# Gated attention and a maxout feed-forward: seven block products on every superblock, half of the turns inside the couple, outputs issued by GpSimd

## The chip, the cores and the metric

The kernel runs on one core of a Trainium2 chip. Its time is the device time of one execution in microseconds; the number that counts is the median over several runs. TensorE is the matrix engine (PE, its weight loads PEld), VectorE is DVE, ScalarE is ACT, GpSimd is POOL, and SyncE (SP) only issues transfers here. Each engine works through its own queue in order, and waits on semaphores where it needs another engine's result.

## The reference

```python
# u, v: 8 x 3072 x 256, z: 8 x 3072 x 64, f32
scores = (1.0 / S) * np.matmul(z, z.transpose(0, 2, 1))
attn = np.maximum(scores, 0.0) ** 2
x = u * np.matmul(attn, v)
# x as 24576 tokens of 256
h1, h2 = x @ w1, x @ w2              # 256 x 1024 each
out = np.maximum(h1, h2) @ w_out     # 1024 x 256
```

Two identities are used by both kernels. The scores are symmetric, so only the blocks on and above the diagonal are computed. And max(h1, h2) = h2 + relu(h1 - h2), so that out = relu(x (w1 - w2)) w_out + x (w2 w_out), where w1 - w2 (`w15_sb`) and w2 w_out (`W2o_sb`) are made once.

## The kernel before

**Tiling.** A batch's 3072 tokens are 24 tiles of 128; four tiles make a group (512 tokens), two groups a *couple* (1024 tokens), so a batch has six groups and three couples c = 0, 1, 2. The attention matrix of a batch is 6 x 6 *blocks* of 512 x 512, kept in bf16 in 27 slots (`free`, `Block`); two by two blocks make a *superblock* (c, o), with blocks A11, A12, A21, A22.

**Scores.** `score_pair` computes half a block: two matmuls at the same time on the two halves of the array's rows (64 is the depth of z), two relus by ScalarE into `r_sb` (three buffers), and later, in `finish`, the square by VectorE into the block. A block above the diagonal is turned by a transposing transfer on SP's queue (`mirror`), which yields its mirror image; of a diagonal block only the upper triangle is computed (a *triangle* pair has less work) and the rest turned in place by three small transfers. A batch has 42 pairs; each couple of the loop issues 14 of them for later use, spread over its steps by `at_step`. `emit_pair(wait=6)` puts the square six steps behind its matmuls in program order.

**Attention times v.** In batch 0 the product is done plainly. From batch 1 on, a couple computes its 1024 x 256 outputs by a scheme of Strassen's kind: on a superblock off the diagonal, eight block products become seven, with sums of score blocks S1 to S4 and of v blocks (`combine_v`) made by VectorE beforehand. On the diagonal superblock the eight plain products stay. `ORDER` lists the products by two lanes, one for each half of the array's rows; one *step* is two matmuls, one per lane. A product is accumulated in one PSUM bank (`BANK`), half of it in one lane and half later in the other; a `nop` on another engine (`relay`) passes on that the first half is done. S1, S2, S3 are made before the couple; S4 overwrites A12 during the couple. The `after_...` functions add up the products in f32 on VectorE (`h_sb`) as they end, and so free the banks.

**Feed-forward.** `gate` multiplies the sums by u (turned by a transposing transfer, `turn_u`) into `xT`, on VectorE. `ff` then does a group: eight times two matmuls into `d_ps`, a relu into `g_sb` (numbers 2, 5 and 7 by VectorE, the others by ScalarE), then for each 128 tokens two matmuls with `W2o_sb` and eight with `w_out_sb` into `o_ps`, a copy by ScalarE into `o_sb` (two buffers) and an output transfer of 256 KB on ScalarE's queue. `d_ps`, `o_ps` and the score tiles share four PSUM buffers; the other four banks belong to the products.

**Order.** The program order is written out by hand. After the steps of couple i come the gates of couple i and the sums for couple i + 1 as a list of VectorE *tasks*, and then, in `second(i - 1, tasks)`, the feed-forward of the couple before. So TensorE has two groups of feed-forward to do while VectorE works on the tasks. `second` spreads the tasks over the feed-forward's matmuls by its `hook`:

```python
places = {(1, 0): 1, (1, 3): 1, (2, 0): 1, (2, 1): 1, (2, 2): 1, (2, 3): 1}
```

so that the relus of VectorE come between them in its queue.

## Time and profile before

| | |
|---|---|
| median of 3 runs | 950.33 us (946.04, 950.33, 955.08) |
| span of the profiled execution | 943.4 us |
| TensorE busy | 929.3 us, 7,706 matmuls |
| VectorE busy | 717.3 us |
| ScalarE busy | 552.8 us |
| GpSimd busy | 57.0 us |
| mean busy share of the 16 DMA engines | 60.4% transposing queue, 20.6% GpSimd's, 8.1% ScalarE's outputs |
| HBM read and written | 59.77 MB and 25.17 MB |

The profile is of one execution, and its span of 943.4 us is the time that the sums below are made against; the page gives no other time for that execution. The timed runs lie 2.6 to 11.7 us above the span. A busy share is an average; what a place costs is read from the timeline at that place.

### The profile page before, as it was taken

The page shows a single profiled execution, that of the slowest core. Times are in us where ns is not written, and L with a number is a line of the kernel's source. Part 1 is how long each engine was busy: PE and PEld are TensorE (multiplying, and loading weights), DVE is VectorE, ACT ScalarE, POOL GpSimd, SP SyncE. Part 2 cuts the span into 40 slices and gives each one's busy share as a digit, 9 for nine tenths or more (in the row PEclk, how much of TensorE's full clock was granted, in tenths as well). Part 3 has the DMA queues.
Part 4 walks back from the last instruction along what each step waited for, and adds up shares of the span by engine and source line. Part 5 has one row for each costly group of instructions (what it writes and reads, how often), then busy time and mean ns, then how long its engine had stood idle before and what let it go on. Part 6 is the DMA issues. An engine that isn't in the chain of part 4 may idle for free.

```text
span 943.4 us, 19492 instructions
## 1 busy us (share of the span) xinstructions
PE 929.3 (99%) x7706; PEld 517.5 (55%) x7706; DVE 717.3 (76%) x1158; ACT 552.8 (59%) x1062; POOL 57.0 (6%) x111
## 2 busy tenths in 40 slices
PE   8997999999999999999999999999999999999998
PEld 4454465554555555555546555465465554655555
DVE  6772588778887787987878869788688787885651
ACT  6793856556556566566565565655756657563333
POOL 3100000000000000000000000000000000000000
PEclk9998999999999999999999999999999999999999
DMA  9999999989999995998979999799979889985301
GB/s 190 148 201 210 164 209 157 133 162 186 148 166 143 159 205 119 174 160 159 185 127 157 164 173 182 119 180 151 172 165 134 172 158 174 153 156 106 80 24 67
DMA packets 388652, 146.00 MB, mean 155 GB/s; under 512 B 361936, under 2 KB 365904, under 8 KB 388560
## 3 DMA queue, kind: packets, MB, share of 16 engines
q1 hardware_dynamic: 359328, 90.09, 60.4%
q0 software_dynamic: 15408, 29.50, 20.6%
q10 hardware_dynamic: 13824, 25.17, 8.1%
q8 instruction: 60, 0.98, 0.5%
q14 instruction: 32, 0.26, 0.1%
HBM read 59.77 MB, written 25.17 MB: 90 GB/s over the span
## 4 chain that ended last, share of the span: by engine, by line
PE 91%; DVE 5%; ACT 1%; issue 1%; DMA 1%; SPq 0%; ACTq 0%; DVEq 0%
PE acc L829 44%; PE o_ps L448 16%; PE d_ps L420 15%; PE s_ps L201 7%; PE o_ps L440 4%; PE acc L259 4%; DVE xT L404 1%; DVE g_sb L428 1%; ACT r_sb L214 1%; DMA blk<-blk 1%; DVE h_sb L735 1%; DVE blk L311 1%; DVE blk L303 0%; DVE blk L307 0%; DVE blk L222 0%
## 5 line engine op out<-in xcount | busy, mean ns | idle before, releaser
L829 PE MATMUL acc<-blk,v_sb 64*128 64x512 bf16 x2544 | 467.1, 376 | 0.0
L214 ACT ACTIVATE r_sb<-s_ps 128x512 bf16<-128x512 f32 (+3 forms) x664 | 333.5, 554 | 127.3 <-PE s_ps L201 126.4
L829 PE MATMUL acc<-blk,vt 64*128 64x512 bf16 x1344 | 328.6, 376 | 0.0
L829 PEld LDWEIGHTS <-v_sb 64*128 64x128 bf16 x2544 | 183.7, 94 | 141.5 <-issue 4.6
L222 DVE TENSOR_TENSOR blk<-r_sb 128x1024 bf16<-128x1024 bf16 x251 | 171.1, 689 | 99.5 <-ACT r_sb L214 98.1
L448 PE MATMUL o_ps<-w_out_sb,g_sb 128*128 128x256 bf16 x1536 | 202.9, 273 | 1.2 <-DVE g_sb L428 0.4
L420 PE MATMUL d_ps<-xT,w_sb 128*128 128x512 bf16 x768 | 180.3, 382 | 5.2 <-ACT o_sb L456 3.9
L448 PEld LDWEIGHTS <-g_sb 128*128 128x128 bf16 x1536 | 150.0, 98 | 26.7 <-DVE g_sb L428 7.0
L829 PEld LDWEIGHTS <-vt 64*128 64x128 bf16 x1344 | 125.6, 94 | 70.7
L456 ACT COPY o_sb<-o_ps 128x512 f32<-128x512 f32 x96 | 56.3, 586 | 184.2 <-PE o_ps L448 174.5
L432 ACT ACTIVATE g_sb<-d_ps 128x512 bf16<-128x512 f32 x240 | 130.3, 599 | 56.8 <-PE d_ps L420 52.3
L420 PEld LDWEIGHTS <-w_sb 128*128 128x128 bf16 x768 | 73.4, 98 | 100.7 <-issue 24.7
L428 DVE TENSOR_SCALAR g_sb<-d_ps 128x512 bf16<-128x512 f32 x144 | 96.2, 685 | 42.6 <-PE d_ps L420 34.2
L201 PE MATMUL s_ps<-zT 64*128 64x512 bf16 (+3 forms) x672 | 124.1, 357 | 1.0 <-ACT zT L119 0.5
L735 DVE TENSOR_TENSOR h_sb<-h_sb,acc 128x512 f32<-128x512 f32 x147 | 96.9, 682 | 28.1 <-PE acc L829 27.4
L220 DVE TENSOR_TENSOR blk<-r_sb 128x512 bf16<-128x512 bf16 (+3 forms) x170 | 50.9, 324 | 41.8 <-ACT r_sb L214 40.7
L440 PE MATMUL o_ps<-W2o_sb,xT 128*128 128x256 bf16 x384 | 73.4, 273 | 0.0
L404 DVE SCALAR_TENSOR_TENSOR xT<-h_sb,uT 128x512 bf16<-128x512 f32 x96 | 63.3, 681 | 0.0
L201 PEld LDWEIGHTS <-zT 64*128 64x128 bf16 x672 | 35.1, 94 | 38.5 <-ACT zT L119 1.0
L259 PE MATMUL acc<-blk,v_sb 64*128 64x512 bf16 x384 | 50.6, 376 | 1.8 <-DVE blk L222 1.3
L311 DVE TENSOR_TENSOR blk<-blk,blk 128x2048 bf16<-128x2048 bf16 x42 | 51.4, 1223 | 1.2
L754 DVE TENSOR_TENSOR blk<-blk,blk 128x2048 bf16<-128x2048 bf16 x42 | 51.1, 1218 | 0.0
(53 smaller groups left out, 348.6 us busy)
## 6 DMA issues: line engine op xcount, KB each, us to landing
out_dram<-o_sb ACTq DMA_DIRECT2D x96, 256.0 KB, 2.8
un<-in_u_dram POOLq DMA_DIRECT2D x48, 256.0 KB, 6.8
v_sb<-in_v_dram POOLq DMA_DIRECT2D x21, 512.0 KB, 7.3
blk<-blk SPq DMA_TRANSPOSE x246, 5.5
zn<-in_z_dram POOLq DMA_DIRECT2D x21, 128.0 KB, 4.5
v_sb<-in_v_dram POOLq DMA_DIRECT2D x6, 256.0 KB, 7.1
blk<-in_moe_w_dram POOLq DMA_DIRECT2D x2, 512.0 KB, 6.2
uT<-un SPq DMA_TRANSPOSE x48, 3.4
```

The lines of the kernel that those rows point to most:

```text
L201: nc.tensor.matmul(s_ps[h][:, lo[h] :], zT[rows, z_at(b, blk * G + tiles[h]), :], zT[rows, q + lo[h] // P : q + G, :].rearrange("p t c -> ...
L214: nc.scalar.activation(o, s, AF.Relu)
L222: nc.vector.tensor_mul(a[:, k : k + 2, :], r, r)
L259: nc.tensor.matmul(a.out(acc[half, dc]), v_at(b, t, dc)[rows], a.moving(rows, j), start=first, stop=last,)
L404: lambda dc=dc: nc.vector.scalar_tensor_tensor(out=x[:, dc, :].rearrange("p (t r) -> p t r", r=P), in0=hs[dc].rearrange("p (t r) -> p t r" ...
L420: nc.tensor.matmul(d_ps, w15_sb[:, kc, ts(nb, P)], xT[:, kc, :], start=(kc == 0), stop=(kc == KD - 1),)
L428: nc.vector.tensor_single_scalar(out=g_sb[:, nb, :], in_=d_ps, scalar=0.0, op=ALU.max)
L432: nc.scalar.activation(g_sb[:, nb, :], d_ps, AF.Relu)
L440: nc.tensor.matmul(o_ps[:, t, :], xT[:, dc, ts(t0 + t, P)], W2o_sb[:, dc, :], start=(dc == 0), stop=False,)
L448: nc.tensor.matmul(o_ps[:, t, :], g_sb[:, nb, ts(t0 + t, P)], w_out_sb[:, nb, :], start=False, stop=(nb == KF - 1),)
L735: nc.vector.tensor_add(out, a, b_)
L829: mm = nc.tensor.matmul(a.out(acc[name]), w()[rows], a.moving(rows, j), start=name not in opened, stop=left[name] == 0,)
```

## The change

The diagonal superblock is now treated like the others, with seven products, so that a couple of batch 1 and later has seven products over three superblocks: P1, X11, P5, P6, P7, X12 and Y (Y0 and Y1 are its two halves, in two banks). Its S1 to S4 mix turned with unturned blocks, which `combine` does with a strided view. v's own difference b12 - b11 is written in place. The order of the superblocks is `FORM_ORDER`, the diagonal one last. S3 is made within the couple (steps 6, 14, 22), S4 at steps 30, 37 and 42. Blocks with equal parity off the diagonal are turned (`late`) within the couple that uses them, from step 36 on; the others as before. Turning u moves to the start of the couple, loading it to the couple before.

`second` issues all tasks ahead of the feed-forward. From batch 1 on all relus of the feed-forward are ScalarE's; for batch 0's couples VectorE keeps numbers 2, 5 and 7. The W2o matmuls of all four tiles come ahead of those with `w_out_sb`. Outputs are issued by GpSimd from three buffers (by SP for the last couple), and the relays go to ScalarE. The sums hold four f32 tiles (`hpool`) for five.

```diff
-    hpool = ctx.enter_context(tc.tile_pool(name="hpool", bufs=5))
+    hpool = ctx.enter_context(tc.tile_pool(name="hpool", bufs=4))
...
-    opool = ctx.enter_context(tc.tile_pool(name="opool", bufs=2))
+    opool = ctx.enter_context(tc.tile_pool(name="opool", bufs=3))
...
+
+    def combine(op, out, x, y):
+        if out.turned == x.turned == y.turned:
+            op(out.ap, x.ap, y.ap)
+            return
+        view = lambda t: t.ap.rearrange(
+            "p (a b r) -> p a b r" if t.turned == out.turned else "p (a b r) -> p b a r",
+            a=G,
+            r=P,
+        )
+        op(view(out), view(x), view(y))
...
-        t = tpool.tile([P, 4, G, P], bf16, name="vt")
+        t = tpool.tile([P, 3, G, P], bf16, name="vt")
...
         return [
-            lambda: nc.vector.tensor_sub(t[:, 0], b12, b11),
-            lambda: nc.vector.tensor_sub(t[:, 2], b22, b12),
-            lambda: nc.vector.tensor_sub(t[:, 1], b22, t[:, 0]),
-            lambda: nc.vector.tensor_sub(t[:, 3], b21, t[:, 1]),
+            lambda: nc.vector.tensor_sub(t[:, 1], b22, b12),
+            lambda: nc.vector.tensor_sub(b12, b12, b11),
+            lambda: nc.vector.tensor_sub(t[:, 0], b22, b12),
+            lambda: nc.vector.tensor_sub(t[:, 2], b21, t[:, 0]),
         ]
...
+                elif b and g // 2 != blk // 2 and g % 2 == blk % 2:
+                    late.append((b, g, blk))
+                    late.sort(key=lambda block: (block[0], block[1] // 2, block[1] % 2))
...
+    FORM_ORDER = ((1, 2, 0), (0, 2, 1), (0, 1, 2))
...
+        forms, s12, s3s = {}, [], []
+        for o in FORM_ORDER[c]:
...
-                nc.vector.tensor_add(f["S1"].ap, f["A21"].ap, f["A22"].ap)
+                combine(nc.vector.tensor_add, f["S1"], f["A21"], f["A22"])
+
+            def s2(f=f):
+                f["S2"] = Block(f["A21"].turned)
+                combine(nc.vector.tensor_sub, f["S2"], f["S1"], f["A11"])

             def s3(f=f):
                 f["S3"] = f["A21"]
-                nc.vector.tensor_sub(f["S3"].ap, f["A11"].ap, f["A21"].ap)
...
-            tasks += [s1, s2, s3]
...
-    ORDER = (
-        (("P1", "P6", "P7", "X11"), ("X11", "P1", "P6", "P7")),
-        (("D22", "X12", "P5", "X21"), ("P5", "X21", "D22", "X12")),
...
+            s12 += [s1, s2]
+            s3s += [s3]
+        return forms, s12, s3s
...
+    LANES = (
+        ("X11", "P5", "P1", "P6", "P7", "Y0", "X12"),
+        ("P1", "P6", "X11", "P5", "X12", "Y1", "P7"),
     )
-    BANK = {"P1": 0, "P6": 1, "P7": 2, "X11": 3, "D22": 0, "P5": 1, "X21": 2, "X12": 3}
+    BANK = {"P1": 0, "P7": 0, "X11": 1, "X12": 1, "P5": 2, "Y0": 2, "P6": 3, "Y1": 3}
...
+    PRODUCTS = {
+        "P1": ("A11", "11"),
+        "X11": ("A12", "21"),
+        "Y0": ("A22", "T4"),
+        "Y1": ("A22", "T4"),
+        "P5": ("S1", "12"),
+        "P6": ("S2", "T2"),
+        "P7": ("S3", "T3"),
+        "X12": ("S4", "22"),
     }
...
-    def ff(b, g, xT, last=False, hook=lambda *at: None):
...
-            if nb in (2, 5, 7):
+            if nb in on_dve:
                 nc.vector.tensor_single_scalar(
                     out=g_sb[:, nb, :], in_=d_ps, scalar=0.0, op=ALU.max
                 )
             else:
                 nc.scalar.activation(g_sb[:, nb, :], d_ps, AF.Relu)
-            hook(1, nb)
...
+        o_ps = {}
         for t0 in range(0, G, 2):
-            o_ps = mm_psum.tile([P, 2, D], fp32, name="o_ps", tag="mm")
-            o_sb = opool.tile([P, 2, D], fp32, name="o_sb")
+            o_ps[t0] = mm_psum.tile([P, 2, D], fp32, name="o_ps", tag="mm")
             for t in range(2):
                 for dc in range(KD):
                     nc.tensor.matmul(
-                        o_ps[:, t, :],
+                        o_ps[t0][:, t, :],
                         xT[:, dc, ts(t0 + t, P)],
                         W2o_sb[:, dc, :],
-                        start=(dc == 0),
+                        start=(t == 0 and dc == 0),
                         stop=False,
                     )
+        for t0 in range(0, G, 2):
+            o_sb = opool.tile([P, 2, D], fp32, name="o_sb")
+            for t in range(2):
                 for nb in range(KF):
                     nc.tensor.matmul(
-                        o_ps[:, t, :],
+                        o_ps[t0][:, t, :],
                         g_sb[:, nb, ts(t0 + t, P)],
                         w_out_sb[:, nb, :],
                         start=False,
-                        stop=(nb == KF - 1),
+                        stop=(t == 1 and nb == KF - 1),
                     )
-                hook(2, t0 + t)
-            nc.scalar.copy(o_sb, o_ps)
-            nc.scalar.dma_start(out=dst[:, ds(t0, 2), :], in_=o_sb)
+            nc.scalar.copy(o_sb, o_ps[t0])
+            queue = nc.sync if last else nc.gpsimd
+            queue.dma_start(out=dst[:, ds(t0, 2), :], in_=o_sb)

...
-                for g, k in ((1, 0), (1, 1), (0, 0), (0, 1)):
+                for g, k in ((1, 0), (0, 1), (1, 1), (0, 0)):
...
-        def second(i, tasks, sums=None):
-
+        def second(i, tasks):
             b, c = couples[i]
-            tasks = list(tasks)
-            places = {(1, 0): 1, (1, 3): 1, (2, 0): 1, (2, 1): 1, (2, 2): 1, (2, 3): 1}
-
-            def hook(stage, n):
-                for _ in range(places.get((stage, n), 0)):
-                    if tasks:
-                        tasks.pop(0)()
-
+            for task in tasks:
+                task()
             for q in range(2):
                 g = 2 * c + q
-                ff(b, g, xTs.pop((b, g)), hook=hook)
-            while tasks:
-                tasks.pop(0)()
+                ff(b, g, xTs.pop((b, g)), on_dve=() if b else (2, 5, 7))
...
-            forms, sums = prepare(b, c)
-            return forms, list(gates) + sums[:3] + tasks + sums[3:]
+            forms, s12, s3s = prepare(b, c)
+            return forms, list(gates) + s12[:4] + tasks + s12[4:], s3s
...
-                at_step.setdefault(2 + n * (len(steps) - 2) // max(n_pairs, 1), []).append(n)
+                first = 10 if b and c else 2
+                at_step.setdefault(first + n * (len(steps) - first) // max(n_pairs, 1), []).append(n)
...
+                h["c"] = new_h()
+                add(h["c"], h["1"], acc["X11"])

             def after_p6():
-                h["U2"] = new_h()
-                add(h["U2"], h["1"], acc["P6"])
+                add(h["1"], h["1"], acc["P6"])
+                h["5"] = new_h()
+                add(h["5"], h["1"], acc["P5"])
...
+            def after_y():
+                h["y"] = new_h()
+                add(h["y"], h["1"], acc["Y0"])
+                add(h["y"], h["y"], acc["Y1"])
...
             def after_p7():
-                h["U3"] = new_h()
-                add(h["U3"], h["U2"], acc["P7"])
...
+                add(h["1"], h["5"], acc["P7"])
+                add(h["5"], h["5"], acc["X12"])
+                add(h["y"], h["y"], acc["P7"])
...
-                nc.vector.tensor_sub(f["A12"].ap, f["A12"].ap, f["S2"].ap)
                 f["S4"] = f["A12"]
-                f["S2"].release()
...
+                combine(nc.vector.tensor_sub, f["S4"], f["A12"], f["S2"])
...
+            if b:
+                assert [ends[n] for n in ("P1", "X11", "P5", "P6", "Y0", "Y1")] == [36, 36, 48, 48, 72, 72]
+                for n, do in (
+                    *zip((6, 14, 22), s3s),
+                    (30, lambda: s4(f[0])),
+                    (36, after_p1),
+                    (37, lambda: s4(f[1])),
+                    (42, lambda: s4(f[2])),
+                    (48, after_p6),
+                    (72, after_y),
+                    (84, after_p7),
+                ):
+                    events.setdefault(n, []).append(do)
...
+            if b:
+                turns = ((0, lambda: turn_u(b, q1)), (1, lambda: turn_u(b, q2)))
...
+            if i + 1 < len(couples):
+                nb_, nc_ = couples[i + 1]
+                for n, q in ((44, 2 * nc_), (50, 2 * nc_ + 1)):
+                    events.setdefault(n, []).append(lambda q=q: load_u(nb_, q))
...
+                if late and s in (36, 40, 48, 54, 60, 66, 72, 78) and free and late[0][:2] in ((b, q1), (b, q2)):
+                    mirror(*late.pop(0))
...
-                        relay = nc.gpsimd.nop()
-                        tc.add_manual_dep(relay.ins, mm.ins.name, AFTER, reason="half done")
-                        relays[marks[s, half]] = relay
+
+                        def relay(mm=mm, name=marks[s, half]):
+                            relays[name] = nc.scalar.nop()
+                            tc.add_manual_dep(
+                                relays[name].ins, mm.ins.name, AFTER, reason="half done"
+                            )
+
+                        events.setdefault(s + 4, []).append(relay)
...
-            out4 = ("1", "U2", "U3", "V") if b else ("D11", "D12", "D21", "D22")
+            if b:
+                while late and late[0][:2] in ((b, q1), (b, q2)):
+                    mirror(*late.pop(0))
+            out4 = ("c", "5", "y", "1") if b else ("D11", "D12", "D21", "D22")
```

## The prediction

> **What bounds the kernel now.** I read the page first: busy time, then the chain that ended last.
>
> ```profile
> PE 929.3 (99%) x7706; PEld 517.5 (55%) x7706; DVE 717.3 (76%) x1158; ACT 552.8 (59%) x1062; POOL 57.0 (6%) x111
> PE 91%; DVE 5%; ACT 1%; issue 1%; DMA 1%; SPq 0%; ACTq 0%; DVEq 0%
> ```
>
> TensorE works 929.3 of 943.4 us and carries 91% of the chain. The windows of one batch (three couples) say how near the others are, in columns of span, PE, PEld, DVE, ACT, POOL:
>
> ```profile
> 225.00:262.00 37.00, 36.95 (x310) 20.73 (x308) 31.60 (x52) 22.14 (x44) 2.65 (x5) 1.00 0.91 151
> 262.00:300.00 38.00, 37.94 (x321) 21.84 (x319) 31.82 (x56) 22.24 (x45) 2.12 (x4) 1.00 1.05 164
> 300.00:338.00 38.00, 37.95 (x318) 20.50 (x316) 29.11 (x43) 23.18 (x44) 1.59 (x3) 1.00 0.98 170
> ```
>
> TensorE has no idle time here, so matmuls removed here are saved in full and every new wait is paid in full. VectorE is second: 92.5 of 113 us, in order, so it can be late at a given place while free on average. The price of its work (groups by form):
>
> ```profile
> L735 DVE TENSOR_TENSOR h_sb<-h_sb,acc 128x512 f32<-128x512 f32 x147 | 96.9, 682 | 28.1 <-PE acc L829 27.4
> L428 DVE TENSOR_SCALAR g_sb<-d_ps 128x512 bf16<-128x512 f32 x144 | 96.2, 685 | 42.6 <-PE d_ps L420 34.2 <-issue 4.6 <-ACT o_sb L456 3.8
> L754 DVE TENSOR_TENSOR blk<-blk,blk 128x2048 bf16<-128x2048 bf16 x42 | 51.1, 1218 | 0.0
> ```
>
> Back to back these follow each other faster than their durations. From the timelines of TensorE, VectorE and ScalarE in one couple:
>
> ```profile
> 323.06 0.38 PE L829 MATMUL acc<-blk,vt 64*128 64x512 bf16 x1
> 324.14 0.38 PE L829 MATMUL acc<-blk,vt 64*128 64x512 bf16 x1
> ...
> 329.52 0.68 DVE L735 TENSOR_TENSOR h_sb<-h_sb,acc 128x512 f32<-128x512 f32 x1
> 330.12 1.22 DVE L754 TENSOR_TENSOR blk<-blk,blk 128x2048 bf16<-128x2048 bf16 x1
> 331.25 0.68 DVE L222 TENSOR_TENSOR blk<-r_sb 128x1024 bf16<-128x1024 bf16 x1
> 331.85 0.68 DVE L735 TENSOR_TENSOR h_sb<-h_sb,acc 128x512 f32<-128x512 f32 x1
> ...
> 326.28 1.08 ACT L214 ACTIVATE r_sb<-s_ps 128x512 bf16<-128x512 f32 x2 [0.43 <-PE s_ps L201]
> 327.25 0.59 ACT L739 COPY h_sb<-acc 128x512 f32<-128x512 f32 x1
> ```
>
> Five steps take 1.08 us: one step (two half-row matmuls at once), and one score pair too, is a slot of 0.2155 us. VectorE's pitch is 0.60 for an add, a square or a relu and 1.13 for a block operation; an operation on the result just before costs 0.06 (add) to 0.12 (block) more. ScalarE does a pair's two relus in 1.08, then a copy. The one large stall stands in batch 0:
>
> ```profile
> 75.11 1.46 PE L420 MATMUL d_ps<-xT,w_sb 128*128 128x512 bf16 x6
> 79.79 0.59 ACT L456 COPY o_sb<-o_ps 128x512 f32<-128x512 f32 x1 [6.08 <-DMA blk<-blk]
> 80.42 1.01 PE L420 MATMUL d_ps<-xT,w_sb 128*128 128x512 bf16 x2 [3.86 <-ACT o_sb L456]
> 82.16 3.57 PE L420 MATMUL d_ps<-xT,w_sb 128*128 128x512 bf16 x8 [0.72 <-ACT g_sb L432]
> 85.52 0.45 PE L440 MATMUL o_ps<-W2o_sb,xT 128*128 128x256 bf16 x2
> 81.00:86.00 5.00, 4.28 (x14) 1.59 (x12) 0.93 (x2) 2.77 (x5) 0.00 (x0) 0.54 1.12 253
> ```
>
> ScalarE was held by its own output transfer, released by a block transpose; 16 matmuls took 10.41 us where the same phase takes 3.63 elsewhere: 6.8 lost. Of that 3.86 is idle; most of the other 2.9 is the granted clock, 0.54 in the last row.
>
> **The change, part by part.** *Products.* Seven products of 12 steps are 84 steps, before 88. 21 couples x 4 x 0.2155 = **-18.1**.
>
> *Output transfers.* Off ScalarE's queue, the 6.8 above goes: **-6.8** (0 if the buffer wait stays). The price: the GpSimd transfers of u, 256 KB as these are, land after a median of 6.8 us against 2.8. With three buffers the fourth copy of a couple, 16.2 us after the feed-forward begins, waits for the first transfer, issued at 6.9: 9.3 us of cover, hence 0; without it ScalarE would be held at the couple's start. The other GpSimd loads behind it are needed a couple later. The Trainium skill (SBUF — State Buffer, section SBUF: two separate sides) warns of this move: descriptors written by GpSimd starve while VectorE runs a two-port copy. The trace shows no sign: the 48 issues of u span 528 to 561 ns beside a VectorE that is 82% busy. By the page a 0.62 us transfer can take 3.1; the sum would still be 0.
>
> *Feed-forward from batch 1.* All eight relus go to ScalarE, at a pitch of 0.535 (five in 2.74 us), against 0.431 for TensorE's two matmuls; the eight W2o matmuls now come first and cover it. The two units of a couple take 3.47 + 4.58 and 3.63 + 4.46 = 16.14 us. The shortest phases in the trace are 3.46 and 4.37, so 15.66 for two; I add 0.1 and 0.2 for the third output-side PSUM buffer waiting for relu 5. 21 x (15.96 - 16.14) = **-3.8**. Bounds: -10.1 without any wait; +14 if each relu takes its full 0.6.
>
> *Relus behind the tasks, twice.* Batch 0 keeps relus 2, 5 and 7 on VectorE, but `second` now issues all tasks ahead of the matmuls instead of spreading them. In (0,1)'s feed-forward (tasks for couple (1,0)) VectorE starts its gates at 116.82 in this trace's time: 4 gates 2.4, three S1/S2 pairs 3 x (1.13 + 0.12 + 1.13) = 7.1, 12 v-combinations at 0.37 = 4.4, so relu 2 starts at 130.7 and, 0.69 long, ends at 131.4. TensorE, which has four PSUM buffers, three of them held by these relus, stops at the second W2o group, at 119.1 (3.71 for the phase, 0.43 for the first group, 0.1 of waiting after 114.87): **12.3**. In (0,2)'s: adds end 2.25 after the couple, gates 2.4, S pairs 7.1, z copies 1.0, relu at 12.8 to 13.5; TensorE stops at 3.98: **9.5**. No cover: nothing else is ready on TensorE. Together **+21.8** (bounds 18 to 25). Both idle times exceed the 3.86 above, which cost 2.9 in clock: **+5.8** (0 to 8). The Trainium skill (TensorE: Matmul & The Clock Gate, part 1) puts the gate at about 3.4 us idle to half rate and 3.4 us busy back; by that the loss would be 1.7 each, 3.4 in all.
>
> *VectorE inside the couple.* It loses six relus (6 x 0.60) and gains four block operations (4 x 1.13): +0.9 a couple on 30.8. Adds stay eight, gates four. What matters is where. From step 30 on the program order is: S4; at 36 the copy of P1 by ScalarE, then c = P1 + X11; at 37 and 42 two S4; at 48 the adds of P6 and P5, between them squares. Y0 and Y1 take P5's and P6's banks at step 60. In couple 2 a pair is issued before step 36, at slot 36 + 5 = 41, 8.84 us in. ScalarE starts 0.41 later, and its copy, behind both relus, ends at 10.81. VectorE: add 10.85, square 11.45, S4 12.05, square 13.18, S4 13.78, square 14.91, P6 15.51, P5 16.17, end 16.85. TensorE would be at step 60 at slot 70, 15.09; it waits **1.8** (part of it at step 56, for S4). Couple 1 has triangles (relus 0.55 a pair, smaller squares): end 16.0 against 14.76, **1.2**. Couple 0 has no pair at 36, copy at 9.05, end 14.84: 0, with 0.2 to spare. Six batches x 3.0, and 0.8 in the last, which has few pairs: **+18.8** (0 if the chain were 1.8 shorter, 35 if it were 1 us longer in all three).
>
> *At no cost.* Diagonal superblocks combine a turned with an unturned block; no row has that. The nearest, the v-combinations with 128-element runs, take 415 ns against 423 contiguous, so I take 1.22; the far bound, the f32 add's 0.60 per 512, makes 2.4, +1.2 on four operations. The transposes keep their number; half of couple 0's move to steps 36 to 54. The one needed first, (1,3)'s, is third in SP's queue and waits for no earlier landing; at 2 to 3 us an issue and 5.5 to land it is there about 22 us into the couple; VectorE reads it at 25.6. A late one would hold S1, S2, then step 12 of the next couple, with 1.7 us more cover. Late or not, its wait would stand on VectorE with S1, S2 and the z copies behind it, not with relus, which are ScalarE's by then. u is loaded at steps 44 and 50 of the couple before and turned at steps 0 and 1, so the gates find it earlier than now; the load waits only for that couple's own turn, some 40 steps back. The relays that let a product change halves move from GpSimd, where they would queue behind outputs, to ScalarE: that of step 15 stands behind a pair's relus, over at 4.9 us, for a matmul due at slot 27, 5.8; if ScalarE were a whole pair late (1.08), TensorE would wait 0.2. The last four outputs go by SP, whose queue is empty then.
>
> Sum: -18.1 - 6.8 - 3.8 + 21.8 + 5.8 + 18.8 = **+17.7**, 943.4 to 961.1 in the profiled span. The runs' median of 950.33 (946.04 to 955.08) lies 6.9 above this span; with the same distance, **968.0**.
>
> **Rivals.** *The lag does not reach TensorE* (other side, not slower): place, steps 52 to 60 of couples 1 and 2; price 18.8; it decides when the work between P1's copy and P5's add is 1.8 us shorter than 6.0. For it: VectorE has 18% idle. Against: the pitches are measured, and the copy stands behind the relus. Time 968.0 - 18.8 = 949.2. With the feed-forward at its bound too (6.3 less) 942.9, and without clock loss 937.1: the way to faster.
> *Mixed layouts run at half speed*: S4 of the diagonal is third and comes before both adds. +1.2 in couples 1 and 2, 1.0 in couple 0, 7 x 3.4 = 23.8, and two operations in each of the two stalls, 4.8: 996.6. Against: the 415 ns row.
> *Late turns*: all seven transposes of couple 0 queue at 4.4 us each, as four do in 17.42 at 63.97; (1,3) lands near 31, inside the cover. At 36 it would cost 7 x 3 = 21: 989.0.
>
> **How the numbers follow.** Forecast 0.62, no lag 0.22, mixed layouts 0.08, late turns 0.08. One per cent, about what a measurement of this kernel can tell from no change, is 940.8 to 959.8. No-lag gives 0.08 of faster and 0.14 of same; the forecast's own range, 955 to 982, puts 0.09 more into same. Faster 0.08, same 0.23, slower 0.69. The range runs from 943, the no-lag case with the feed-forward at its bound, to 986, a forecast with the lag at its bound (16.2 more) and a little over.
>
> **What would show it.** Steps right: L829's line with 3,720 matmuls. Two TensorE waits of 9 to 13 us on a VectorE relu near 112 and 165, with a granted clock near 0.5 behind them. In couples 1 and 2, TensorE waiting for an add or block operation, 1 to 2 us each, none in couple 0. No 3.86 wait near 80. I am wrong if TensorE is unbroken from batch 1 on, if those two waits are missing, or if block operations on the diagonal exceed 1.3 us.

## The result, and the profile after

The changed kernel takes 997.88 us (median of four runs, 988.02 to 1008.14) against 948.18 us for the kernel before on the same chip: 1.050 times as long, 95% interval 1.042 to 1.057. The prediction was 968.0, range 943 to 986: right in direction, wrong in size. The profiled execution is the shortest of the four, 988.02 us with a span of 986.2; the sum was made for the span, +17.7, and the span grew by 42.8. (Ratios here leave out runs over 1.5% above the fastest of their kernel, so they are not always the quotient of the medians.)

The page first: busy time, then the chain that ended last.

```profile
PE 917.9 (93%) x7490; PEld 520.9 (53%) x7538; DVE 735.2 (75%) x1116; ACT 594.7 (60%) x1167; POOL 108.0 (11%) x203
PE 76%; DVE 14%; DMA 6%; issue 3%; ACT 1%; SPq 0%; DVEq 0%; ACTq 0%
```

TensorE's work fell by 11.4 us, but it now carries 76% of the chain instead of 91; VectorE and transfers have taken the rest. Whom TensorE waits for (total, times, longest):

```profile
PE o_ps L443 <- DVE g_sb L432: 28.8, 2, 16.1
PE s_ps L212 <- DMA zT<-zd: 10.5, 6, 3.2
PE acc L827 <- DVE h_sb L737: 7.4, 11, 0.9
PE acc L827 <- DMA blk<-blk: 4.6, 1, 4.6
PE acc L827 <- DVE blk L130: 3.3, 6, 0.8
PE acc L827 <- DVE blk L123: 1.7, 4, 0.5
```

The first row is the two stalls that the prediction named, in TensorE's timeline:

```profile
132.19 1.01 PE L443 MATMUL o_ps<-W2o_sb,xT 128*128 128x256 bf16 x4 [12.75 <-DVE g_sb L432]
187.09 1.01 PE L443 MATMUL o_ps<-W2o_sb,xT 128*128 128x256 bf16 x4 [16.06 <-DVE g_sb L432]
```

The second and fourth row end in turns of SP's queue, which the prediction had put at no cost. VectorE waits for such turns far longer than TensorE does. From the groups (busy time, mean ns, idle time ahead and who ended it):

```profile
L827 PE MATMUL acc<-blk,v_sb 64*128 64x512 bf16 x2208 | 401.1, 380 | 9.5 <-DMA blk<-blk 4.6
L827 PE MATMUL acc<-blk,vt 64*128 64x512 bf16 x1512 | 316.3, 379 | 7.7 <-DVE h_sb L737 6.8
L123 DVE TENSOR_TENSOR blk<-blk,blk 128x2048 bf16<-128x2048 bf16 x168 | 202.2, 1221 | 63.3 <-DMA blk<-blk 54.9
L130 DVE TENSOR_TENSOR blk<-blk,blk 128x2048 bf16<-128x2048 bf16 x84 | 102.5, 1220 | 2.4 <-DMA blk<-blk 1.7
```

2,208 + 1,512 are the 3,720 matmuls foreseen. L130 is the strided view of a diagonal superblock, and takes what L123, the plain one, takes: the rival of mixed layouts falls here. The new reading is the 54.9 us in the third line.

A table by stage shows where the time lies. Each stage runs from its first matmul to the next stage's first, in us from the trace; c0 to c2 are the sums over batches 1 to 6 (c0 from batch 2, and of batch 7), six couples each. Four later kernels, described below, stand beside it.

| stage | before | changed | relus | slots | three | best |
|---|---|---|---|---|---|---|
| start, batch 0 | 65.67 | 65.30 | 65.26 | 66.41 | 65.33 | 65.55 |
| feed-forward of (0,0) | 23.19 | 16.16 | 15.81 | 16.31 | 15.82 | 15.82 |
| couple (0,2) | 24.82 | 32.30 | 38.82 | 37.40 | 27.02 | 25.77 |
| feed-forward of (0,1) | 16.57 | 30.67 | 15.75 | 31.09 | 15.74 | 15.74 |
| couple (1,0) | 21.80 | 20.94 | 20.93 | 20.94 | 20.94 | 20.94 |
| feed-forward of (0,2) | 16.14 | 33.83 | 15.75 | 30.28 | 15.75 | 15.75 |
| c0, six | 130.82 | 125.64 | 127.49 | 125.63 | 125.61 | 127.49 |
| c1, six | 128.88 | 140.95 | 145.02 | 131.77 | 124.47 | 124.50 |
| c2, six | 132.72 | 146.30 | 141.85 | 139.72 | 140.83 | 128.57 |
| (7,1) and (7,2) | 39.18 | 38.59 | 38.38 | 38.38 | 37.44 | 37.67 |
| all other feed-forwards, 21 | 338.77 | 330.41 | 330.61 | 330.65 | 330.65 | 330.40 |

### The profile page after: what moved, and what is told of

It reads as the page before. It is cut to its first block, busy times and chain, and to the rows that moved or that the text cites. A ratio compares the mean times of both kernels' runs of the same rounds, so it can differ in the third digit from the quotient of the medians.

```text
span 986.2 us, 19236 instructions
## 1 busy us (share of the span) xinstructions
PE 917.9 (93%) x7490; PEld 520.9 (53%) x7538; DVE 735.2 (75%) x1116; ACT 594.7 (60%) x1167; POOL 108.0 (11%) x203
## 4 chain that ended last, share of the span: by engine, by line
PE 76%; DVE 14%; DMA 6%; issue 3%; ACT 1%; SPq 0%; DVEq 0%; ACTq 0%
PE acc L827 32%; PE o_ps L454 15%; PE d_ps L424 15%; PE s_ps L212 5%; DMA blk<-blk 4%; PE o_ps L443 4%; DVE blk L123 4%; PE acc L273 4%; DVE blk L130 3%; DVE blk L233 2%; DMA zT<-zd 2%; DVE h_sb L737 2%; DVE blk L231 1%; ACT r_sb L225 1%; DVE zd L143 0%
## 5 line engine op out<-in xcount | busy, mean ns | idle before, releaser
L827 PE MATMUL acc<-blk,v_sb 64*128 64x512 bf16 x2208 | 401.1, 380 | 9.5 <-DMA blk<-blk 4.6
L123 DVE TENSOR_TENSOR blk<-blk,blk 128x2048 bf16<-128x2048 bf16 x168 | 202.2, 1221 | 63.3 <-DMA blk<-blk 54.9
L827 PEld LDWEIGHTS <-v_sb 64*128 64x128 bf16 x2208 | 157.4, 95 | 125.3 <-issue 10.9
L436 ACT ACTIVATE g_sb<-d_ps 128x512 bf16<-128x512 f32 x366 | 185.8, 623 | 29.7 <-PE acc L827 17.3
L454 PE MATMUL o_ps<-w_out_sb,g_sb 128*128 128x256 bf16 x1536 | 177.8, 275 | 0.0
L424 PE MATMUL d_ps<-xT,w_sb 128*128 128x512 bf16 x720 | 167.5, 379 | 2.6 <-issue 0.2
L454 PEld LDWEIGHTS <-g_sb 128*128 128x128 bf16 x1536 | 151.5, 99 | 18.8
L737 DVE TENSOR_TENSOR h_sb<-h_sb,acc 128x512 f32<-128x512 f32 x168 | 113.3, 685 | 41.1 <-PE acc L827 19.5
L212 PE MATMUL s_ps<-zT 64*128 64x512 bf16 (+3 forms) x672 | 129.7, 360 | 12.2 <-DMA zT<-zd 10.5
L463 POOL DMA_DIRECT2D out_dram<-o_sb x92 | 50.4, 547 | 608.6 <-ACT o_sb L461 608.6
L130 DVE TENSOR_TENSOR blk<-blk,blk 128x2048 bf16<-128x2048 bf16 x84 | 102.5, 1220 | 2.4 <-DMA blk<-blk 1.7
L443 PE MATMUL o_ps<-W2o_sb,xT 128*128 128x256 bf16 x384 | 50.9, 275 | 29.5 <-DVE g_sb L432 28.8
L443 PEld LDWEIGHTS <-xT 128*128 128x128 bf16 x384 | 37.8, 98 | 45.1 <-issue 30.6
```

The source lines that it names most:

```text
L123: op(out.ap, x.ap, y.ap)
L130: op(view(out), view(x), view(y))
L212: nc.tensor.matmul(s_ps[h][:, lo[h] :], zT[rows, z_at(b, blk * G + tiles[h]), :], zT[rows, q + lo[h] // P : q + G, :].rearrange("p t c -> ...
L424: nc.tensor.matmul(d_ps, w15_sb[:, kc, ts(nb, P)], xT[:, kc, :], start=(kc == 0), stop=(kc == KD - 1),)
L436: nc.scalar.activation(g_sb[:, nb, :], d_ps, AF.Relu)
L443: nc.tensor.matmul(o_ps[t0][:, t, :], xT[:, dc, ts(t0 + t, P)], W2o_sb[:, dc, :], start=(t == 0 and dc == 0), stop=False,)
```

## The experiments

Four suspects stand in the table: the relus left on VectorE, an order inside the couples, the turns, and the end of batch 0. All times are compared with the kernel before on the same chip (947.47, 947.95, 944.46 and 946.45 us in the four groups of runs).

### Three of them, one by one and together

*The relus of batch 0.*

```diff
-                ff(b, g, xTs.pop((b, g)), on_dve=() if b else (2, 5, 7))
+                ff(b, g, xTs.pop((b, g)), on_dve=())
```

> The changed kernel, with the relus of batch 0's two feed-forwards that VectorE takes (stages 2, 5 and 7) given to ScalarE, as they already are from batch 1 on. Theory T1 (those relus queue behind VectorE's list of gates, sums and squares, which is now issued before the feed-forward): the waits of o_ps at line 443, 12.75 us at 132.19 and 16.06 us at 187.09, go down to under 1 us each, the half-clock stretches behind them (13.65 and 17.07 us) go with them, and the execution ends 28 to 33 us earlier: 955 to 960 us for 988. Rival R1 (VectorE's list is what is late, not the relus in it; without them TensorE waits for the same list at its next consumer, the couple that follows): the waits move to line 827 of couples (0,2) and (1,0) and the time falls by under 12 us.

964.81 us, ratio 1.013 (1.004 to 1.023), 33 us below the changed kernel, though above the 955 to 960 expected. Both feed-forwards fall to 15.75 (column "relus"), and no wait of o_ps is left. T1 holds: the relus were in the wrong queue, and nothing behind VectorE's list is needed at once. The profiled span fell by only 25.4, since couple (0,2) happened to take 38.82, on which more below.

*The order inside the couples.*

```diff
+                    (33, lambda: s4(f[1])),
                     (36, after_p1),
-                    (37, lambda: s4(f[1])),
-                    (42, lambda: s4(f[2])),
+                    (37, lambda: s4(f[2])),
...
+                first_do = b and s == 36      # copy of P1 ahead of the score pair
```

> The changed kernel, with two orders altered inside a couple of batches 1 to 7: the second and third S4 are issued at steps 33 and 37 rather than 37 and 42, and at step 36 the copy of P1 and the sum of it and X11 are issued ahead of the score pair. Theory T2 (VectorE's and ScalarE's queue order is what makes TensorE wait about steps 48 to 60, a fixed lag): couples 1 and 2, at best 21.95 and 23.20 us against 20.69 and 21.12 unstalled, come down to within 0.5 us of these in their best batches, and the kernel is 15 to 20 us faster than the changed one. Rival R2 (VectorE is short of time in these stages and any order only moves the wait): best couples stay above 21.8 and 23.0 and the time moves by under 5 us.

991.44 us, ratio 1.044 (1.036 to 1.052), beside 1.050 (1.042 to 1.057) for the changed kernel: the runs do not tell the two apart, and neither theory is whole. The best couple 1 takes 20.75, unstalled, as T2 says; the best couple 2 takes 21.70, and 0.27 of that is a wait for z. But the others take 22.5 to 27.5 us. In couples 1 VectorE comes late for another reason; in couples 2 TensorE waits for VectorE no more, but for z, up to 4.4 us.

*The slots.*

```diff
         A[b, blk, g] = t
+        turning.append(A[b, g, blk].ap)
         A[b, g, blk].release()
...
+            recent = [id(ap) for ap in turning[-7:]]
+            free.sort(key=lambda ap: recent.index(id(ap)) if id(ap) in recent else -1)
             forms, s12, s3s = prepare(b, c)
```

> The changed kernel, with the list of free slots sorted before a couple's S1 and S2 take theirs, so that the seven slots freed last by a turn are taken last. Theory T3 (VectorE's waits for a turned block are mostly waits to overwrite a slot that a queued turn still reads): VectorE's waits for those transfers, 54.9 us in 17 in the changed kernel, fall to under 20 us, the wait of o_ps at 187 us falls from 16.1 to 9 to 11 us, couples 1 and 2 lose most of what they have over their best batches (16 us in all), and the kernel is 12 to 22 us faster than the changed one. Rival R3 (VectorE reads the turned block itself before it has landed; the slot doesn't matter): the waits stay above 40 us and the time moves by under 5 us.

976.06 us, ratio 1.028 (1.021 to 1.035): 22 us better in the medians, for a reordered list. T3 holds. VectorE's waits for turns in this kernel, to be read against the 54.9 above:

```profile
DVE blk L123 <- DMA blk<-blk: 12.3, 7, 3.8
```

All six couples 1 now take 21.96 or 21.97, the base lag of 1.26 over 20.69 and nothing more; all couples 2 but one take 23.22 or 23.23. What happened in the changed kernel is seen in VectorE's queue behind couple (2,0) and in SP's at the same time:

```profile
305.50 1.23 DVE L123 TENSOR_TENSOR blk<-blk,blk 128x2048 bf16<-128x2048 bf16 x1 [2.55 <-DMA blk<-blk]
313.88 3.62 DVE L123 TENSOR_TENSOR blk<-blk,blk 128x2048 bf16<-128x2048 bf16 x3 [7.15 <-DMA blk<-blk]
319.81 0.89 DVE L143 COPY zd<-zn 128x512 bf16<-128x512 bf16 x4
297.47 16.71 SPq L257 DMA_TRANSPOSE blk<-blk  x5
320.33 2.79 SPq L144 DMA_TRANSPOSE zT<-zd  x2
```

The short wait is S1's for the block that it reads. The long one is S2's: it writes to the slot taken first from the free list, which was the source of a turn still in SP's queue. Program order had given the slot back when the turn was issued, but the chip has to read it first. In the kernel with the sorted list the same S2 waits for no turn. In the feed-forward of (0,2) the wait of o_ps falls from 16.06 to 11.98, not to the 9 to 11 expected: VectorE still waits there 2.78 us for a turn before S1.

*All three.*

> The three edits together: batch 0's relus on ScalarE, the new order inside the couples, the sorted slots. Theory T4 (the three causes are separate and their prices add up): 988 less 28 to 33, less 15 to 20, less 12 to 22, which is 913 to 933 us, and so faster than the kernel before (its profiled execution spans 943 us). Rival R4 (the causes share VectorE's time; removing one exposes the next): 945 to 960 us.

936.69 us, ratio 0.979 (0.969 to 0.989), so 1 to 3% faster than before. It is 61 us below the changed kernel, and the three medians alone add up to 61 (33 + 6 + 22), but each of these is known only to some 10 us either way, and the median misses T4's 913 to 933, in which two of the four runs lie. By stage the edits do not simply add: the six couples 1 lose 0.9 us by the order alone, 9.2 by the slots alone, and 16.5 by all three. With the slots in order the lag edit does its whole work in couple 1: 20.74 in each batch. Couple 2 stays at 22.1 to 25.4; TensorE waits there for VectorE no more, but for z, 10.5 us in six waits.

### What is left in couple 2, and at the end of batch 0

*Outputs by GpSimd alone, on the kernel before.* This part of the change by itself, first alone, then with the plain blocks of (0,2) reordered.

```diff
-            nc.scalar.dma_start(out=dst[:, ds(t0, 2), :], in_=o_sb)
+            queue = nc.scalar if last else nc.gpsimd
+            queue.dma_start(out=dst[:, ds(t0, 2), :], in_=o_sb)
...
-                b, c, forms, blocks=() if b else (4, 5, 2, 3, 0, 1)
+                b, c, forms, blocks=() if b else (2, 0, 1, 3, 5, 4)    # second kernel only
```

> The kernel before, with one part of the change alone: outputs except the last couple's are issued by GpSimd instead of ScalarE. Theory T5 (what the first feed-forward saves, 7 us, is given back in the couple behind it, because its first block is turned last of batch 0 and SyncE's queue of turns ends no sooner): the feed-forward at 67 us falls from 23.19 to 16 to 17 us, the couple (0,2) rises from 24.82 to 30 us or more, the rest stays, and the kernel is within 0.4% of before (945 to 951 us). Rival R5 (the prediction's own term, a gain that stays): (0,2) stays at 25 us and the kernel is 6 to 8 us faster (ratio 0.992 to 0.994).

> As the last one, and in couple (0,2) the plain blocks are taken in the order 2, 0, 1, 3, 5, 4 for 4, 5, 2, 3, 0, 1, which is the order in which their turned halves are issued, so the block that is turned last is used last. Theory T5: the feed-forward at 67 us takes 16 to 17 us, (0,2) takes 22 to 25 us, and the kernel is 6 to 9 us faster than before (937 to 942 us). Rival R5b (the turns themselves are too few per us for this couple, whatever the order): (0,2) stays above 28 us and the kernel is within 0.4% of before.

977.32 us, ratio 1.031 (1.026 to 1.036), and 973.11, 1.026 (1.021 to 1.032): 25 to 29 us slower, which neither theory expected. On the disputed place T5 is right. The first feed-forward falls from 23.19 to 16.16, and couple (0,2) rises from 24.82 to 35.07; with the new order (0,2) is back at 24.82, but couple (1,0) takes 27.83 for 21.80. So what is saved there is given back in one of the two couples behind. The rest is another loss, in the feed-forwards behind couple 1 of batches 1 to 6: 17.7 to 21.8 us for 16.2. VectorE's gates wait for u there, and its relus stand behind them:

```profile
PE d_ps L420 <- DVE g_sb L428: 13.2, 6, 3.9
DVE xT L404 <- DMA uT<-un: 14.7, 6, 4.2
```

In the change, u is loaded and turned earlier and no relu is on VectorE from batch 1 on, and this loss does not appear. Which of the two prevents it was not tried.

*The block order on the three edits.*

> The three edits together (batch 0's relus on ScalarE, the order inside the couples, the sorted slots) and the same order of blocks in couple (0,2). Its four couples (0,2) so far took 27 to 39 us. Theory T5: (0,2) takes 22 to 25 us in any run, the spread of the runs (926 to 942 us for the three edits) shrinks to under 6 us, and the kernel takes 918 to 926 us. Rival R5b: (0,2) still takes 27 us or more in the profile and the spread stays.

935.19 us, ratio 0.984 (0.979 to 0.989). (0,2) falls to 25.77, but (1,0) takes 33.50, and the runs still spread from 930 to 946: the stall moves on here too, but by another path. In the kernel above VectorE waited 7.1 us for a turn; here TensorE waits 9.4 us for ScalarE, whose copy waits until an earlier output by GpSimd has left its buffer:

```profile
ACT o_sb L462 <- DMA out_dram<-o_sb: 12.0, 1, 12.0
```

T5 is right on the couple, R5b on the spread.

*z turned early.* The last third of the next batch's z was copied at the end of VectorE's list behind couple 1 and turned behind six triangle turns and a block:

```diff
-                if b and b + 1 < B and c < 2:
-                    tasks += [lambda piece=piece: turn_z(b + 1, piece) for piece in ((0, 1), (2,))[c]]
+                if b and b + 1 < B and c < 1:
+                    tasks += [lambda piece=piece: turn_z(b + 1, piece) for piece in (0, 1)]
...
-                    ((20, lambda: load_z(b + 1, 2)), (45, lambda: load_v(b + 1, 2))),
+                    ((6, lambda: load_z(b + 1, 2)), (45, lambda: load_v(b + 1, 2)), (60, lambda: turn_z(b + 1, 2))),
```

> As the last one, and the third part of the next batch's z is loaded at step 6 and turned at step 60 of couple 1, ahead of the six triangle turns that stood before it in SyncE's queue, rather than after that couple. Theory T6 (what is left in couple 2, 22.1 to 25.4 us for 21.12 unstalled, is TensorE's wait for this turn, 10.5 us in six couples, and not VectorE's lag): couple 2 falls to 21.1 to 21.6 us in each batch and the kernel is 10 to 14 us faster than the last one: 906 to 915 us. Rival R6 (another wait of VectorE stands behind it): couple 2 stays above 22.5 us and the time falls by under 4 us.

926.92 us (six runs from 914.29 to 935.79), ratio 0.966 (0.961 to 0.972). Couple 2 takes 21.42 to 21.44 in all six batches. T6 is right on the couple: what was left there, once VectorE's order had been changed, was this queue. It is seen in SP's timeline of the kernel with three edits, where z, copied by 309.7, is issued at 321.2:

```profile
309.33 8.66 SPq L236 DMA_TRANSPOSE blk<-blk  x6
318.09 3.06 SPq L257 DMA_TRANSPOSE blk<-blk  x1
321.24 1.26 SPq L144 DMA_TRANSPOSE zT<-zd  x1
```

Two of the six runs reach T6's 906 to 915. Between the two profiled executions the span falls from 933.5 to 920.4: couples 2 give 9.9 us, and couples (0,2) and (1,0), which change places, give 3.4 together. (1,0) falls from 33.50 to 20.94, but (0,2) rises from 25.77 to 34.91: TensorE waited 7.2 us there for batch 1's z, behind a turn that took 13.47 us to issue.

*The end of batch 0.* Two ways to help that turn, and both together (on the last kernel): v's load later in (0,2), and z's turn ahead of the turn of block (0,1) of batch 1.

```diff
-                    ((10, lambda: load_v(b + 1, 1)),),
+                    ((10 if b else 48, lambda: load_v(b + 1, 1)),),
...
-        second(PLAIN // 2 - 2, tasks + [lambda: turn_z(1, 2)])
+        second(PLAIN // 2 - 2, tasks + [lambda: turn_z(1, 2), lambda: mirror(1, 0, 1)])
```

> The last kernel (relus, order, slots, order of the plain blocks, early z), and in couple (0,2) the load of the next batch's second third of v is issued at step 48 rather than 10. Theory T7 (one turn in SyncE's queue takes 12 to 16 us to issue, 13.5 us at 88.09 in the last kernel and 12.5 us at 83.59 in the changed one, since GpSimd's 512-KB loads of v move at the same time, at 85.0 and 85.3 us; the turns behind it are late): no turn between 78 and 105 us takes over 6 us to issue, (0,2) takes 22 to 25 us, and the kernel takes 908 to 918 us. Rival R7 (the turn waits for something in its own queue): a turn there still takes over 7 us and (0,2) over 27 us in the profile, or the stall moves to couple (1,0).

> The last kernel but with v's load as it was; instead the turn of batch 1's third part of z is issued ahead of the turn of block (0,1) of batch 1 in SyncE's queue. Theory T8 (what stalls couple (0,2) now, 7.2 us, is the order of the queue: z stands behind a turn that nobody needs before couple (1,0)): the wait of s_ps for z is gone, (0,2) takes 22 to 25 us, and the kernel takes 908 to 918 us. Rival R8 (z isn't late by order; the queue as a whole is): the stall moves to another consumer of a turn in (0,2) or (1,0) and the two couples together still take over 52 us (20.94 and 21.8 unstalled).

> Both. T7 or T8: couples (0,2) and (1,0) together take 43 to 47 us, the runs lie within 8 us of each other, and the kernel takes 906 to 916 us, 0.956 to 0.966 of before. R8: over 920 us.

v later: 920.58 us, ratio 0.974 (0.970 to 0.978); z first: 919.60, 0.974 (0.969 to 0.979); both: 913.27, ratio 0.968 (0.966 to 0.970), four runs from 912.9 to 915.1. T7 alone fails: a turn still took 10.87 us, and (0,2) 33.90. T8 alone fails as well: z's wait shrinks to 3.5 us in two and (0,2) takes 31.11. Together (0,2) and (1,0) take 46.7 and TensorE is nearly unbroken. This is the best version, 31 us faster than the kernel before. Its page:

```profile
PE 901.9 (99%) x7490; PEld 518.8 (57%) x7538; DVE 721.1 (79%) x1098; ACT 601.2 (66%) x1185; POOL 107.9 (12%) x203
PE 90%; DMA 3%; issue 3%; DVE 2%; ACT 1%; POOL 0%; ACTq 0%; POOLq 0%; DVEq 0%
```

*Why one turn is long.* First the two loads of u in (0,2) were issued at later steps (without and with z first); then they were made to wait for VectorE, which clears one element of their buffer.

```diff
-                    (2, lambda: load_u(b, q1)),
-                    (6, lambda: load_u(b, q2)),
+                    (36, lambda: load_u(b, q1)),    # third kernel: (44, lambda: load_u(b, q1, held=True))
+                    (40, lambda: load_u(b, q2)),    # and (46, ... held=True)
```

> The kernel whose load of v in couple (0,2) was moved to step 48 (early z, without z ahead of the block's turn), and now the two 256-KB loads of u in that couple, by GpSimd, are issued at steps 36 and 40 rather than 2 and 6, and turned at 64 and 70 rather than 6 and 14. In the kernel without this a turn issued at 88.08 us took 10.87 us, with the loads of u issued at 84.08 and 84.6. Theory T10 (GpSimd's loads and outputs of 256 to 512 KB that move beside a turn make it long, and the u loads alone do): no turn between 78 and 98 us takes over 6 us to issue, (0,2) takes 25 to 26 us as in the kernel with z ahead, and the kernel takes 910 to 915 us. Rival R11 (the turn is long for what stands before it in SyncE's own queue): a turn there still takes over 7 us and TensorE waits for z over 3 us.

> The same two loads of u moved in the kernel that has v late and z ahead (913.3 us). T10: the turn that took 7.48 us there at 85.69 takes under 5 us; TensorE waits for none of it already, so 908 to 914 us. R11: over 6 us again, same time.

> In the last two runs the loads of u still went at 84 us, since GpSimd had nothing to wait for, whatever step issued them. Now they do wait: VectorE clears one element of their buffer at steps 44 and 46 of couple (0,2), so GpSimd's loads of u and v start after about 92 us; z is not ahead. T10: the turn of block (0,1) of batch 1 behind the first z, 8.5 to 13.5 us in three runs with the loads at 84 us, takes under 5 us, and TensorE's wait for z in (0,2) is under 1 us. R11: that turn still takes over 7 us. Its own cost is known from the last two runs: the later loads of u hold GpSimd's outputs and couple (1,0) takes 25 to 33 us, so the total is 915 to 932 us and tells nothing; the turn's own time does.

The first two, 929.32 us (0.981, 0.974 to 0.987) and 925.60 (0.977, 0.969 to 0.984), don't test what they should: GpSimd had nothing to wait for and issued the loads at 84 us all the same. They show something else: the later turn of u holds GpSimd's next load of u, the outputs queue behind that load, and couple (1,0) takes 30.0 and 32.7 us. The third (one run, 925.85 us) does test it, on the turn's own time. SP's timeline, first with the loads of u at 84 us (the kernel with v later), then with them held to 93.8:

```profile
82.97 15.98 SPq L257 DMA_TRANSPOSE blk<-blk  x2
99.05 2.32 SPq L144 DMA_TRANSPOSE zT<-zd  x1
```

```profile
82.63 7.12 SPq L259 DMA_TRANSPOSE blk<-blk  x2
89.85 1.26 SPq L144 DMA_TRANSPOSE zT<-zd  x1
```

The same two turns take 15.98 and 7.12 us to issue (the second of them alone 10.87 and 3.25), and TensorE's wait for z is gone: T10, by one execution of each kernel. It fits that the same turn took 8.51 us in the first of the three kernels, with the loads at 84 us, and 1.79 in the next experiment's, where GpSimd issues nothing at that time. The Trainium skill (DMA: Bandwidth & Descriptors, section SWDGE vs HWDGE vs iDMA) says that the engines behind GpSimd's and SyncE's queues are the same and take turns between them; these rows agree. The run's total tells nothing more: the second clearing itself waited for a turn of u, and (0,2) took 37.94. In the steady state, the long turns (6 to 11 us in several batches) were not traced to a cause one by one.

*Outputs on ScalarE in the new kernel.* The kernel with early z, with one line undone.

```diff
-            queue = nc.sync if last else nc.gpsimd
+            queue = nc.sync if last else nc.scalar
```

> The kernel with early z, but its outputs issued by ScalarE again, as before the change. Theory T9 (outputs on GpSimd save the 7 us of the first feed-forward and nothing in the steady state, and where SyncE's queue is late they give it back): the feed-forward at 67 us takes 23 us for 15.8, the couple (0,2) behind it 22 to 25 us for 34.9, all other feed-forwards 15.75 us, and the kernel is within 5 us of the one with GpSimd's outputs. Rival R9 (GpSimd's transfers slow SyncE's turns, so all couples gain): the kernel is over 8 us faster. Rival R10 (ScalarE's relus of scores and feed-forward fall behind its DMA issues): over 8 us slower.

1003.14 us, ratio 1.061 (1.057 to 1.066). The profiled span is 999.9 us for 920.4, so some 80 us slower: R10's size, though not its reason. The first feed-forward takes 25.3 and (0,2) 25.8, as T9 has it, but the feed-forward behind couple 1 takes 26.9 to 30.0 us in each of batches 1 to 6:

```profile
ACT o_sb L462 <- DMA blk<-blk: 75.2, 7, 13.7
PE d_ps L425 <- ACT o_sb L462: 62.7, 7, 11.9
```

ScalarE waits for turns seven times. In the program each of its output issues carries, beside the wait for its own copy, one on a completion semaphore that SP's turns use as well; with turns queued there an output can't be issued before an unrelated turn has ended, and the relus behind it can't start. (The output issued at 211.74 us, for one, stood behind a wait for the semaphore that a turn issued at 209.23 signals.) In the kernel before this happened once, at 80 us; here it happens in each of batches 1 to 6. That the turns moved into the couple bring it about is likely, but was not tried by itself.

## Why the prediction was wrong, point by point

- *Products, -18.1*: right. Couple 0 takes 20.94 for 21.80 everywhere, four slots less, and 3,720 matmuls are counted.
- *Output transfers, -6.8*: this step failed. The feed-forward lost its 7.0 us, but the couple behind it took 7.5 more. The step asked what held ScalarE, a turn, but not what that turn's queue owed the next consumer: couple (0,2) now begins 7.4 us sooner, while the turn that it begins with is issued at 81.39 us for 83.85, only 2.5 sooner, and TensorE waits 4.6 us for it. On price it erred the other way: GpSimd's outputs land after a median of 2.6 us, not 6.8, and of the interference with VectorE's copies that was weighed there this median shows none. The price that exists is another: GpSimd's transfers lengthen SP's turns (15.98 for 7.12). Nor does the cover of 9.3 us that put the buffer wait at 0 always hold: with the plain blocks reordered ScalarE waited 12.0 us for one output. And the part is worth far more than its term, as cover: without it the kernel with early z loses some 80 us.
- *Feed-forward, -3.8*: -8.4 over 21, 15.75 for 16.14 in most; the 0.3 added for the PSUM buffer was not needed.
- *Relus behind the tasks, +21.8*: right at the first place (12.75 for 12.3), wrong at the second (16.06 for 9.5). The step let VectorE's list run without waiting; it stood 6.9 us for turns, in two waits. The sentence that a late turn would have no relus behind it overlooked that this feed-forward is batch 0's. Without the relus both go, with 33 us.
- *Clock, +5.8*: too much. The windows behind the two stalls (span, PE, PEld, DVE, ACT, POOL, then the granted clock) give

```profile
132.00:145.00 13.00, 12.76 (x87) 9.26 (x88) 4.53 (x7) 4.43 (x8) 1.25 (x3) 0.87 0.25 71
187.00:200.00 13.00, 12.85 (x89) 9.43 (x90) 5.58 (x8) 4.43 (x8) 1.49 (x3) 0.88 0.63 122
```

  13 x 0.13 + 13 x 0.12 = 3.3 us. The estimate of 3.4 by the Trainium skill (TensorE: Matmul & The Clock Gate, part 1) was the better guide than the row of before, which had another small wait in it.
- *VectorE inside the couple, +18.8*: right in size and cause, as far as it goes. Couple 1 loses 1.26 for 1.2 (with the slots in order), and the order of events removes it. Couple 2 loses 2.1 for 1.8 at the least, 23.23 over 21.12. In couple (1,2) of the changed kernel TensorE does not wait for z at all, and in (2,2) it waits 1.53 us; yet in both it goes on 17.1 us into the couple (they begin at 238.10 and 354.99), behind an add of VectorE. The wait for z is hidden in the lag:

```profile
255.17 0.61 PE L827 MATMUL acc<-blk,vt 64*128 64x512 bf16 x4 [0.76 <-DVE h_sb L737]
366.84 0.39 PE L212 MATMUL s_ps<-zT 64*128 64x512 bf16 x2 [1.53 <-DMA zT<-zd]
372.07 0.61 PE L827 MATMUL acc<-blk,vt 64*128 64x512 bf16 x4
```

  In the kernel with the new order and early z the same matmuls of (1,2) start 15.3 us into the couple, 1.8 sooner. So beside the lag z's late turn costs only what exceeds it, and shows in full once the lag is gone. But couples 1 and 2 of batches 1 to 6 lost 36.0 us over the saving of their products (+25.65, where 12 x 0.862 = 10.3 was saved), not 18. About 20 of it is this lag (six times 1.26 and 2.11); the other 16 are waits for turns, and sorting the slots takes nearly all of them away.
- *Late turns, "at no cost"*: this step failed, and cost most. It followed one turn to its reader and found 3.6 us in hand. It did not ask which slot the next sum would write, nor what stood behind the turns in the same queue. The list's order alone was worth 22 us in the medians, 9.2 and 6.6 of it in couples 1 and 2. The rival that I gave 0.08 to, late turns at 21 us and 989.0, named the right queue and nearly the size, but the wrong edge: a slot to be written, not a block to be read. Turning all blocks at once was not tried: 27 slots don't hold them.

The failed terms in the span: outputs +7.3 against the sum, couples 1 and 2 +18.3 (the last batch's among them), relus and their clock +4.2, feed-forward -4.6; together 25.2, for the 25.1 that the sum missed.

## What to carry to other kernels

A buffer that program order calls free may still be read by a transfer in a slow queue; when transfers are moved later, give recently released slots out last, and ask for each transfer what it delays behind it in its own queue as well as who reads it. When a stall is removed from an engine, look for the queue that released it: if that queue ends no sooner, the next consumer pays. And price the parts of a change together: outputs on another engine were a loss alone (+29 us), a small term in the sum, and some 80 us of cover in the new order.

## What was not expected of the hardware

A wait of TensorE well below 3 us can bring the half clock, and one as long can pass without it. In the kernel with three edits, the windows behind a wait of 2.23 us at 210.83 and of 2.21 us at 549.24:

```profile
210.80:214.30 3.50, 3.47 (x18) 1.35 (x20) 1.41 (x3) 1.08 (x2) 0.67 (x2) 0.52 1.04 195
549.20:552.70 3.50, 3.46 (x32) 1.57 (x34) 2.56 (x5) 2.40 (x5) 0.67 (x2) 1.00 1.05 196
```

18 matmuls in the first and 32 in the second, at 0.52 and 1.00 of the clock: the same wait cost 1.7 us more or nothing. The Trainium skill (TensorE: Matmul & The Clock Gate, part 1) says that the gate watches a free-running window, which would let the same wait fall differently; but it names a window of about 3.4 us without work, and these waits were shorter.
